# Splitting the first two modulation rows into four column blocks, and moving first-chunk layer-norm work between ScalarE and VectorE, in a fused adaLN, linear-attention and SwiGLU kernel

## The chip, the cores and the metric

The kernel runs on one core of one Trainium2 chip. The time is the device time of the core in microseconds (us). A kernel is executed several times, and the medians below are over its executions. "Granted clock" is the profile's figure for the share of the full TensorE clock that was granted on average over an execution.

## The reference

The reference is a transformer block with adaptive layer norm on 2048 tokens of width 1024, in bf16. Only the beginning matters here: six modulation rows come from the condition vector `c`, and the first two of them (shift `sa` and scale `ca`) must be known before any attention projection can start.

```
mod = (silu(c) @ w_mod).reshape(1, 6, 1, -1)        # w_mod: 1024 x 6144
sa, ca, ga, sb, cb, gb = mod[:, 0], ..., mod[:, 5]
h = layernorm(x) * (1 + ca) + sa                     # 2048 x 1024
q, k, v = h @ wqkv                                   # 32 heads of 32
... linear attention, @ wo, residual; second layer norm; SwiGLU with F = 3584; residual
```

## The kernel before

All weights are read from memory while the kernel runs. The first chunk of 512 tokens is normalised and transposed on chip; one scale and shift then make it ready for the K projection. The 1024 input channels are eight "channel rows" of 128 (`cc` 0 to 7). The modulation values of a channel row need that row's 128 columns of `w_mod` for both kinds (scale and shift). So the columns are loaded in blocks of channel rows (`PH`), interleaved with the matching rows of the K weights, and the K matmuls of the first chunk follow the blocks as they land. They accumulate in eight PSUM banks at once (`bank[0]` to `bank[7]`), one bank for each group of 128 tokens x 512 columns.

```python
PH = [(0, 2), (2, 5), (5, 8)]                     # blocks of 256, 384, 384 columns
for st in range(STC): load_x(st)
load_wme(0, 0, DC); load_wk(0, 2)                 # modulation block 0, K weights of rows 0, 1
load_wme(1, 0, 4); load_wme(1, 4, 8); load_wk(2, 3); load_wk(3, 5)
load_wme(2, 0, 4); load_wme(2, 4, 8); load_wk(5, 6); load_wk(6, 8)
...                                               # then the V weights (load_cols(wv, ...))

def mod_mm(p, kind, j0, j1):                      # one-column matmuls into columns of bank 7
    ... nc.tensor.matmul(bank[7][:, o:o + 1], lhsT=wme[:, j, col:col + P], rhs=scT[:, j:j + 1], ...)

def phi_to(dst, acc):                             # eviction of one K bank
    nc.scalar.activation(out=e, in_=acc, func=ACT.Exp)
    nc.vector.tensor_scalar(out=e, in0=e, scalar1=1.0, scalar2=PHI_EPS, op0=ALU.min, op1=ALU.add)
    nc.vector.scalar_tensor_tensor(out=dst, in0=acc, scalar=0.0, in1=e, op0=ALU.max, op1=ALU.add)

# ... front: statistics of tiles 0 to 2 on VectorE, tile 0 normalised on ScalarE, then
kblk(range(4), 0)                                 # K matmuls of groups 0..3, channel row 0
tr0(2); tr0_evac(2)                               # transpose of tile 2
# ...
kblk(range(7), 2); kblk(range(7), 3); kblk(range(3), 4)
mod_mm(2, 0, 0, 4); mod_mm(2, 1, 0, 4)
kblk(range(3, 7), 4)
mod_mm(2, 0, 4, 8); mod_mm(2, 1, 4, 8)
mod_finish(2); modulate_phase(2)                  # VectorE: casts, then scale and shift
for cc in range(5): kblk((7,), cc)                # group 7 uses bank 7, free only now
for g in range(8):
    for cc in range(5, 8): kblk((g,), cc)         # three matmuls finish each group
    k_evac(bank[g], *G[g])
# then the V groups, which use banks 0, 1, 2, ... in turn
```

## Time and profile before

| | kernel before |
|---|---|
| median, first three runs | 838.97 us (837.6 to 840.78) |
| span of the profiled run, granted clock | 836.1 us, 1.000 |
| first K matmul | 11.63 us |
| first V matmul | 30.84 us |
| TensorE gaps after 30.84 us | none until the last instructions |

Two lines of the page: the busy times of the engines, and the granted clock in 40 slices.

```profile
PE 829.2 (99%) x4208; PEld 388.7 (46%) x4208; DVE 351.3 (42%) x660; ACT 149.9 (18%) x284; POOL 79.2 (9%) x146
PEclk9999999999999999999999999999999999999999
```

TensorE is the bottleneck. From V's first matmul on it is never without work, so the span is V's start plus a constant of about 805.3 us. Only the first 31 us can change. The timeline of TensorE there follows (start, duration, line, operation; in brackets the idle time and what ended it). L267 are the K matmuls, L363 the one-column modulation matmuls, L282 the V matmuls.

```profile
11.63 1.04 PE L267 MATMUL bank<-M,M 128*128 128x512 bf16 x4 [0.25 <-DVE M L249]
...
15.23 0.82 PE L267 MATMUL bank<-M,M 128*128 128x512 bf16 x3 [0.23 <-DVE M L249]
...
17.69 3.84 PE L267 MATMUL bank<-M,M 128*128 128x512 bf16 x17 [0.24 <-DVE M L249]
21.37 0.74 PE L363 MATMUL bank<-scT,M 128*128 128x1 bf16 x24
21.98 1.02 PE L267 MATMUL bank<-M,M 128*128 128x512 bf16 x4
22.84 0.44 PE L363 MATMUL bank<-scT,M 128*128 128x1 bf16 x12
23.81 0.45 PE L363 MATMUL bank<-scT,M 128*128 128x1 bf16 x12 [0.53 <-DMA M<-in_w_mod_dram]
24.58 6.42 PE L267 MATMUL bank<-M,M 128*128 128x512 bf16 x29 [0.32 <-DVE saT L370]
30.84 13.98 PE L282 MATMUL bank<-M,M 128*128 128x512 bf16 x64
```

After the first K matmul the bracketed waits sum to 1.32 us (0.23 + 0.24 + 0.53 + 0.32). The 0.53 is the wait for the last transfer of the third modulation block, which the chain shows from its issue to its landing (start, duration, what):

```profile
14.77 8.99 DMA M<-in_w_mod_dram
```

Between 21.37 and 24.58 us TensorE is issued 48 one-column matmuls and only four K matmuls.

### The profile page before, as it was taken

To read this page: it belongs to the slowest core of one execution; us is meant where nothing else is said; L and a number is where in the kernel's file an instruction comes from. 1 tells how busy PE (TensorE), PEld (TensorE's weight loads), DVE (VectorE), ACT (ScalarE), POOL (GpSimd) and SP (SyncE) were. 2 spreads that over 40 slices of the span, in tenths; PEclk is the share of its full clock that TensorE was granted. 3 is DMA by queue.
4 is the path that set the end of the run, shared out by engine and by line. 5 is a ranking of instruction groups with operands and counts; after the bars stand their busy time and mean duration, and the time that the engine had idled before them with its cause. 6 is when DMAs were issued, how large, how long until landed. Compare 5 with 4: busy or idle time off the path is not lost.

```text
span 836.1 us, 10576 instructions
## 1 busy us (share of the span) xinstructions
PE 829.2 (99%) x4208; PEld 388.7 (46%) x4208; DVE 351.3 (42%) x660; ACT 149.9 (18%) x284; POOL 79.2 (9%) x146
## 2 busy tenths in 40 slices
PE   8999999999999999999999999999999999999998
PEld 4454544544444444444444444444444444444445
DVE  5758889788656655344552012222101111111111
ACT  3335533313211111111110001111000111100000
POOL 2114300032222223100000000000000000000000
PEclk9999999999999999999999999999999999999999
DMA  9985688154599998998884225555312555211220
GB/s 303 310 184 128 123 174 217 44 133 126 151 215 217 221 230 201 245 283 239 251 267 118 76 73 154 154 155 151 104 66 94 152 153 153 74 38 45 76 70 26
DMA packets 230529, 129.41 MB, mean 155 GB/s; under 512 B 87632, under 2 KB 216656, under 8 KB 230480
## 3 DMA queue, kind: packets, MB, share of 16 engines
q1 hardware_dynamic: 180128, 97.01, 42.2%
q10 hardware_dynamic: 48048, 23.34, 13.0%
q0 software_dynamic: 2304, 8.39, 2.6%
q8 instruction: 33, 0.54, 0.3%
q14 instruction: 16, 0.13, 0.1%
HBM read 95.42 MB, written 12.58 MB: 129 GB/s over the span
## 4 chain that ended last, share of the span: by engine, by line
PE 97%; SPq 2%; DMA 1%; issue 0%; DVE 0%
PE bank L563 23%; PE bank L538 23%; PE bank L544 23%; PE bank L282 7%; PE bank L495 7%; PE bank L290 7%; PE bank L267 6%; DMA M<-in_w_mod_dram 1%; SPq L144 1%; PE bank L468 1%; PE bank L299 1%; SPq L147 0%; SPq L137 0%; PE bank L363 0%; DVE M L566 0%
## 5 line engine op out<-in xcount | busy, mean ns | idle before, releaser
L544 PE MATMUL bank<-M,M 128*128 128x512 bf16 x896 | 211.7, 379 | 0.0
L538 PE MATMUL bank<-M,M 128*128 128x512 bf16 x896 | 211.6, 379 | 0.0
L546 DVE TENSOR_TENSOR M<-bank,e 128x512 bf16<-128x512 f32 x112 | 77.4, 691 | 249.2 <-PE bank L544 244.6
L563 PE MATMUL bank<-M,M 128*128 128x512 bf16 (+2 forms) x728 | 148.0, 363 | 0.0
L541 ACT ACTIVATE e<-bank 128x512 f32<-128x512 f32 x112 | 66.8, 597 | 439.7 <-PE bank L538 409.5
L563 PEld LDWEIGHTS <-M 128*128 128x128 bf16 x952 | 90.9, 98 | 103.0
L544 PEld LDWEIGHTS <-M 128*128 128x128 bf16 x896 | 87.7, 98 | 105.7
L538 PEld LDWEIGHTS <-M 128*128 128x128 bf16 x896 | 87.4, 98 | 103.8
L566 DVE TENSOR_TENSOR M<-bank,M 128x512 bf16<-128x512 f32 (+2 forms) x34 | 22.4, 660 | 169.9 <-PE bank L563 169.9
L267 PE MATMUL bank<-M,M 128*128 128x512 bf16 x256 | 57.4, 379 | 1.0 <-DVE M L249 0.7
L495 PE MATMUL bank<-M,M 128*128 128x512 bf16 x256 | 57.9, 379 | 0.0
L290 PE MATMUL bank<-M,M 128*128 128x512 bf16 x256 | 57.5, 379 | 0.0
L282 PE MATMUL bank<-M,M 128*128 128x512 bf16 x256 | 55.9, 379 | 0.0
L262 ACT ACTIVATE e<-bank 128x512 f32<-128x512 f32 x64 | 37.7, 595 | 86.4 <-PE bank L290 53.0
L563 PE MATMUL bank<-M 128*128 128x512 bf16 x224 | 51.0, 379 | 0.0
L264 DVE SCALAR_TENSOR_TENSOR M<-bank,e 128x512 bf16<-128x512 f32 x64 | 44.3, 692 | 3.9
L322 DVE CUSTOM_DVE_ANT_0 M<-M,sc_bc 128x1024 f32<-128x1024 bf16 x32 | 40.0, 1249 | 0.5
L282 PEld LDWEIGHTS <-M 128*128 128x128 bf16 x256 | 25.0, 98 | 30.2
L495 PEld LDWEIGHTS <-M 128*128 128x128 bf16 x256 | 25.0, 98 | 29.7
L267 PEld LDWEIGHTS <-M 128*128 128x128 bf16 x256 | 24.4, 98 | 29.6 <-DVE M L249 1.8
L263 DVE TENSOR_SCALAR e<-e 128x512 f32<-128x512 f32 x64 | 28.4, 444 | 23.0 <-ACT e L262 22.9
L290 PEld LDWEIGHTS <-M 128*128 128x128 bf16 x256 | 24.6, 98 | 27.8
(72 smaller groups left out, 337.7 us busy)
## 6 DMA issues: line engine op xcount, KB each, us to landing
M<-in_B_w_gate_dram SPq DMA_DIRECT2D x56, 512.0 KB, 3.9
M<-in_B_w_up_dram SPq DMA_DIRECT2D x56, 512.0 KB, 5.0
x_scratch<-M POOLq DMA_DIRECT2D x16, 512.0 KB, 6.0
M<-x_scratch ACTq DMA_DIRECT2D x16, 512.0 KB, 3.5
M<-in_B_w_down_dram SPq DMA_DIRECT2D x6, 1024.0 KB, 8.4
M<-in_A_x_dram SPq DMA_DIRECT2D x16, 256.0 KB, 3.6
M<-in_A_wqkv_dram SPq DMA_DIRECT2D x4, 1024.0 KB, 11.4
M<-in_A_x_dram ACTq DMA_DIRECT2D x16, 256.0 KB, 4.2
```

Of the source, the lines that this page charges most:

```text
L262: nc.scalar.activation(out=e[:], in_=acc, func=ACT.Exp)
L264: nc.vector.scalar_tensor_tensor(out=dst, in0=acc, scalar=0.0, in1=e[:], op0=ALU.max, op1=ALU.add)
L267: nc.tensor.matmul(acc[:], lhsT=M4[:, sc_, cc, t * P:(t + 1) * P], rhs=wk[:, cc, h * NB:(h + 1) * NB], start=(cc == 0), stop=(cc == DC - 1))
L282: nc.tensor.matmul(acc[:], lhsT=M4[:, sc_, cc, t * P:(t + 1) * P], rhs=wv[:, cc, h * NB:(h + 1) * NB], start=(cc == 0), stop=(cc == DC - 1))
L290: nc.tensor.matmul(acc[:], lhsT=wq[:, cc, qc * P:(qc + 1) * P], rhs=M4[:, sc_, cc, :], start=(cc == 0), stop=(cc == DC - 1))
L322: nc.vector.tensor_tensor_reduce(out=prod.rearrange("p (j k) -> p j k", j=DC), in0=rowT[i][:, :, b, :], in1=sc_bc[:].rearrange("p (j k) -> ...
L495: nc.tensor.matmul(acc[:], lhsT=oTs[st % 3][:, cc, :], rhs=wo[:, cc, hs], start=(cc == 0), stop=(cc == DC - 1))
L538: nc.tensor.matmul(g_ps[:], lhsT=wg_blk[:, cc, fs], rhs=M4[:, sc_, cc, :], start=(cc == 0), stop=(cc == DC - 1))
L541: nc.scalar.activation(out=sg[:], in_=g_ps[:], func=ACT.Silu)
L544: nc.tensor.matmul(u_ps[:], lhsT=wu_blk[:, cc, fs], rhs=M4[:, sc_, cc, :], start=(cc == 0), stop=(cc == DC - 1))
L546: nc.vector.tensor_tensor(out=gus[sc_][:, f, :], in0=u_ps[:], in1=sg[:], op=ALU.mult)
L563: nc.tensor.matmul(y_ps[:, 0:w], lhsT=gus[sc_][:, f, t * P:(t + 1) * P], rhs=wd(f)[:, c0:c1], start=(f == 0), stop=(f == FC - 1))
```

## The change: intent and diff

The last block that must arrive before K can end is made small: four blocks of 256, 384, 256 and 128 columns instead of three of 256, 384, 384. Then only one channel row, eight matmuls, remains behind it. In front, the statistics of tile 1 go to ScalarE and tile 0 is normalised on VectorE (tiles 1 to 3 already were), so that tile 2 can be transposed before the first K matmul. The bytes moved are the same.

```diff
-    PH = [(0, 2), (2, 5), (5, 8)]
+    PH = [(0, 2), (2, 5), (5, 7), (7, 8)]
@@ loads
     load_wk(5, 6)
-    load_wk(6, 8)
+    load_wk(6, 7)
+    load_wme(3, 0, DC)
+    load_wk(7, 8)
@@ front (warm(19) became warm(21))
-    for st in range(3):
-        ln_stats(st)
-    ln_xn(0)
+    ln_stats(0)
+    ln_stats_act(1)
+    ln_stats(2)
+    ln_xn(0, nc.vector)
     tr0(0)
     tr0_evac(0)
     warm(2)
-    ln_xn(1, nc.vector)
+    ln_stats(3, lambda: ln_xn(1, nc.vector))     # between the two halves
     tr0(1)
     tr0_evac(1)
-    ln_stats(3)
+    ln_xn(2, nc.vector)
     mod_mm(0, 0, 0, DC)
     mod_mm(0, 1, 0, DC)
-    warm(3)
     mod_finish(0)
+    tr0(2)
+    tr0_evac(2)
     modulate_phase(0, 0, 2 * P)
-    for st in (2, 3):
-        ln_xn(st, nc.vector)
+    ln_xn(3, nc.vector)
@@ K of the first chunk (order of the second block's part cut here)
     kblk(range(7), 2)
     kblk(range(7), 3)
-    kblk(range(3), 4)
     mod_mm(2, 0, 0, 4)
     mod_mm(2, 1, 0, 4)
-    kblk(range(3, 7), 4)
+    kblk(range(4), 4)
     mod_mm(2, 0, 4, 8)
     mod_mm(2, 1, 4, 8)
     mod_finish(2)
     modulate_phase(2)
+    kblk(range(4, 7), 4)
+    kblk(range(7), 5)
+    kblk(range(4), 6)
+    mod_mm(3, 0, 0, DC)
+    mod_mm(3, 1, 0, DC)
+    mod_finish(3)
+    modulate_phase(3)
     spread(nc.vector, scT[:])
-    for cc in range(5):
+    kblk(range(4, 7), 6)
+    for cc in range(7):
         kblk((7,), cc)
     for g in range(8):
-        for cc in range(5, 8):
-            kblk((g,), cc)
+        kblk((g,), 7)
         k_evac(bank[g], *G[g])
```

More of the change, by code (lines that the diff above doesn't have):

```diff
@@ L196, with ln_stats @@
     stat = {}
-    def ln_stats(st):
+    def ln_stats(st, between=None):
         x_sb = xs[st % 6]
@@ L201, in ln_stats @@
         for i in range(NH):
+            if i == 1 and between is not None:
+                between()
             nc.vector.bn_stats(out=stats[:, i, :], in_=x_sb[:, i * NB:(i + 1) * NB])
@@ L378, in modulate_phase @@
             modulate(0, cc, saT, ca1T, c0, c1)
-    warm(19)
+    warm(21)
     mask = const.tile([P, KVW], BF16, name="mask")
@@ L417 @@
     kblk(range(4), 0)
-    tr0(2)
-    tr0_evac(2)
-    kblk(range(2), 1)
+    kblk(range(1), 1)
     tr0(3)
     tr0_evac(3)
-    kblk(range(2, 4), 1)
+    kblk(range(1, 4), 1)
     modulate_phase(0, 2 * P, 4 * P)
+    kblk(range(4, 6), 0)
     mod_mm(1, 0, 0, 4)
     mod_mm(1, 1, 0, 4)
-    kblk(range(4, 7), 0)
+    kblk(range(6, 7), 0)
+    kblk(range(4, 5), 1)
     mod_mm(1, 0, 4, 8)
@@ L431 @@
     modulate_phase(1)
-    kblk(range(4, 7), 1)
+    kblk(range(5, 7), 1)
     kblk(range(7), 2)
     kblk(range(7), 3)
-    kblk(range(3), 4)
     mod_mm(2, 0, 0, 4)
     mod_mm(2, 1, 0, 4)
-    kblk(range(3, 7), 4)
+    kblk(range(4), 4)
     mod_mm(2, 0, 4, 8)
```

## The prediction

> **What bounds the kernel.** The busy times give TensorE 829.2 of 836.1 us; the clock is 1.00. The timeline shows no TensorE gap after 24.58 us, where the last key (K) matmuls of the first chunk begin; V begins at 30.84. The change touches only the time before that. It pays one for one if V starts earlier, and nothing otherwise.
>
> There, three limits alternate. (1) DMA: busy share 1.08 to 1.10 in every 5 us window from 5 to 25; transfers land in queue order: first modulation block 10.11, first K weights 11.48, second block 16.28, third 23.76, first V weights 28.78 us. (2) The chain "last modulation matmul, casts, modulate on VectorE, K matmul": 16.64 to 17.69, 1.05 us. (3) TensorE itself: from 11.63 to 30.84 it has 64 K matmuls of 0.216, two transposed tiles (0.9) and 96 small matmuls (2.5): 17.2 of 19.2 us. Only some 2 us are waits, so that is the ceiling; one more tile transposed before 11.63 could add 0.45.
>
> **What the change does.**
> - Bytes are unchanged, packets shorter. Medians in the trace: 768 B take 40 ns, 512 B 27 ns, 256 B (transposing loads elsewhere) 18 ns. The third block falls to 1 MB at 512 B, about 3.4 us (estimate); the last, 0.5 MB at 256 B, about 2.1 us against 1.6 at 768 B. [...] Estimates: third block 22.5 (was 23.76), fourth 26.0, last K weights 26.7, V weights 29.7 us (was 28.78).
> - Front: normalising tile 0 on VectorE (0.54 us) for ScalarE (1.24) waits behind tile 2's statistics, so it ends near 7.5 instead of 7.66. Tile 1's statistics on ScalarE take 1.05+0.2+0.2+1.15+0.2, then three POOL steps of 1.3: ready near 8.5, as now. The first K matmul stays near 11.6, because its weights land at 11.48. Little is gained.
> - Middle: tile 3's copy and modulate now leave TensorE about 0.7 us idle near 14; the small matmuls that filled this come later. Third channel block: 17.85 instead of 17.69.
> - End: 18 instead of 29 matmuls follow the last modulation matmuls, but these come near 26.5 instead of 24.2. K ends near 30.5.
> - New: the final row is one matmul per group (0.216) instead of three (0.65), so bank 0 finishes only near 29.1 us; its exp, min/add and max/add take 1.8 us (26.50 to 28.28 before). V's first group uses bank 0, so V starts near 31.0. The eight evictions end near 38.4 instead of 35.7, on VectorE, with slack: the second chunk's modulation ended 3 us before it was needed.
>
> Thus the waits removed (about 1) are paid back by this eviction and new waits. Net +0.2 us by the sum, with an error of 0.6; small against the runs' spread (837.6 to 840.78).
>
> **Prediction: 838.9 us, range 836.9 to 841.0. Faster by over 2%: 0.005; within 2%: 0.985; slower: 0.01.**
>
> **Right if** the profile shows: first K matmul 11.4 to 11.8; the fourth block landing 25.5 to 26.7; V weights 29.3 to 30.3; V's first matmul 30.3 to 31.3, after a short wait for bank 0's eviction; no TensorE waits later; no more ScalarE table loads than now.
>
> **Wrong if** 256 B packets cost far more than 18 ns (each us moves V's start); if Copy and Square need a table load (1.28 us), delaying tile 1; if the later eviction delays the second chunk's transposes enough to stop TensorE near 60 us; or if the small matmuls fill waits better than I count, giving a start near 29.7 (1 us faster).

The transfer times of 3.4, 2.1 and 1.6 us are estimates; the packet medians beside them give much the same over the 16 DMA engines of the page (2048 x 27 ns, 2048 x 18 ns and 683 x 40 ns, divided by 16: 3.5, 2.3 and 1.7 us).

## The result and the profile after

| | before | after |
|---|---|---|
| median of six runs | 839.39 us (837.6 to 840.78) | 838.2 us (838.03 to 838.74) |
| span of the profiled run, clock | 836.1 us, 1.000 | 837.0 us, 1.000 |
| first K matmul | 11.63 us | 11.51 us |
| first V matmul | 30.84 us | 31.44 us |

The ratio after to before is 0.999, with a 95% interval of 0.9976 to 1.0004: the same. Ratios in this document are the mean time of one kernel's fast runs over that of the other's in the same rounds, so they are not quite the ratios of the medians.

There is a contradiction to explain. The median fell by 1.2 us, but the profiled run became 0.9 us longer, 0.6 us of it because V starts later. First the profile. The page's busy times, then TensorE's timeline; L271 are now the K matmuls, L367 the one-column matmuls, L286 the V matmuls. (Some matmul records are missing from the trace, so counts can be short by a few.)

```profile
PE 825.1 (99%) x4127; PEld 388.4 (46%) x4207; DVE 351.5 (42%) x660; ACT 150.9 (18%) x288; POOL 80.1 (10%) x147
```

```profile
11.51 1.25 PE L271 MATMUL bank<-M,M 128*128 128x512 bf16 x4 [0.32 <-DVE M L253]
...
14.45 0.61 PE L271 MATMUL bank<-M,M 128*128 128x512 bf16 x2 [0.59 <-DVE M L253]
...
17.59 1.69 PE L271 MATMUL bank<-M,M 128*128 128x512 bf16 x7 [0.46 <-DVE M L253]
19.75 1.67 PE L271 MATMUL bank<-M,M 128*128 128x512 bf16 x7 [0.48 <-DMA M<-in_A_wqkv_dram]
21.26 0.54 PE L367 MATMUL bank<-scT,M 128*128 128x1 bf16 x16
21.66 1.02 PE L271 MATMUL bank<-M,M 128*128 128x512 bf16 x4
22.52 0.81 PE L367 MATMUL bank<-scT,M 128*128 128x1 bf16 x16
23.41 0.59 PE L271 MATMUL bank<-M,M 128*128 128x512 bf16 x2
24.24 2.55 PE L271 MATMUL bank<-M,M 128*128 128x512 bf16 x11 [0.24 <-DVE M L253]
26.63 0.54 PE L367 MATMUL bank<-scT,M 128*128 128x1 bf16 x16
27.03 4.04 PE L271 MATMUL bank<-M,M 128*128 128x512 bf16 x18
31.44 13.76 PE L286 MATMUL bank<-M,M 128*128 128x512 bf16 x61 [0.36 <-DVE M L268]
```

The wait for the modulation transfer (0.53 us) is gone, and the K matmuls behind the last block fell from 29 to 18. But the waits after the first K matmul now sum to 2.13 us (0.59 + 0.46 + 0.48 + 0.24 + 0.36). Some of these have other causes than before: 0.59 us for tile 3's scale and shift, which 24 one-column matmuls had filled before; 0.48 us for K weights whose slowest part landed at 19.71 us (19.04 before); and 0.36 us between K and V. The chain of waits shows what the last one is (start, duration, what):

```profile
14.85 8.09 DMA M<-in_w_mod_dram
...
29.60 0.61 ACT e L266
30.23 0.44 DVE e L267
...
30.69 0.70 DVE M L268
...
31.44 0.59 PE bank L286 x2
```

These three instructions are the eviction of bank 0 (the reading of its finished sums), the bank that V's first group needs. In the kernel before it ran from 26.50 to 28.28 us, under K matmuls. Now each group is finished by a single matmul in the last row, so bank 0 is finished only near 29.6 us. Its eviction takes 1.8 us and ends after K does.

The trace's completion times of the transfers answer the other part of the prediction: third block 22.93 us, fourth block 26.04, V weights 29.67 (28.78 before). The packets of 256 bytes took 18 ns in the median, those of 512 bytes 27 ns.

### The profile page after: what moved, and what is told of

The parts are those of the page before. It is cut to its first block, busy times and chain, and to the rows that moved or that the text cites. A ratio compares the mean times of both kernels' runs of the same rounds, so it can differ in the third digit from the quotient of the medians.

```text
span 837.0 us, 10504 instructions
## 1 busy us (share of the span) xinstructions
PE 825.1 (99%) x4127; PEld 388.4 (46%) x4207; DVE 351.5 (42%) x660; ACT 150.9 (18%) x288; POOL 80.1 (10%) x147
## 4 chain that ended last, share of the span: by engine, by line
PE 96%; SPq 2%; DMA 1%; issue 1%; DVE 0%; ACT 0%
PE bank L555 23%; PE bank L574 23%; PE bank L549 23%; PE bank L286 7%; PE bank L506 7%; PE bank L294 7%; PE bank L271 6%; DMA M<-in_w_mod_dram 1%; PE bank L479 1%; PE bank L303 1%; SPq L144 1%; SPq L147 1%; SPq L137 0%; PE bank L367 0%; DVE M L268 0%
## 5 line engine op out<-in xcount | busy, mean ns | idle before, releaser
L577 DVE TENSOR_TENSOR M<-bank,M 128x512 bf16<-128x512 f32 (+2 forms) x34 | 22.5, 661 | 169.9 <-PE bank L574 153.8
L271 PE MATMUL bank<-M,M 128*128 128x512 bf16 x248 | 56.8, 379 | 2.6 <-DVE M L253 1.6
L286 PE MATMUL bank<-M,M 128*128 128x512 bf16 x251 | 55.6, 379 | 0.6 <-DVE M L268 0.4
L286 PEld LDWEIGHTS <-M 128*128 128x128 bf16 x256 | 25.0, 98 | 30.8 <-issue 0.6
L271 PEld LDWEIGHTS <-M 128*128 128x128 bf16 x256 | 24.1, 98 | 30.8 <-DVE M L253 3.3
L294 PEld LDWEIGHTS <-M 128*128 128x128 bf16 x256 | 24.6, 98 | 27.9
```

What stands on the lines that cost most here:

```text
L271: nc.tensor.matmul(acc[:], lhsT=M4[:, sc_, cc, t * P:(t + 1) * P], rhs=wk[:, cc, h * NB:(h + 1) * NB], start=(cc == 0), stop=(cc == DC - 1))
L286: nc.tensor.matmul(acc[:], lhsT=M4[:, sc_, cc, t * P:(t + 1) * P], rhs=wv[:, cc, h * NB:(h + 1) * NB], start=(cc == 0), stop=(cc == DC - 1))
L294: nc.tensor.matmul(acc[:], lhsT=wq[:, cc, qc * P:(qc + 1) * P], rhs=M4[:, sc_, cc, :], start=(cc == 0), stop=(cc == DC - 1))
```

## The experiments

Twelve kernels ran, in three sessions of four, each on another chip, called A, B and C here. Five executions were asked for each, beside nine of the kernel before in the same session; every execution has its own mean granted clock. One question is where V starts, which one profile for each kernel answers for that execution: two profiles of one kernel differ by 0.03 to 0.32 us (before and e8_before, after and e11_after, e1_tail and e12_tail). The other is why the executions of one kernel differ by up to 3 us.

| profiled run | V starts, us | span, us | span minus V's start |
|---|---|---|---|
| before | 30.84 | 836.1 | 805.3 |
| after | 31.44 | 837.0 | 805.6 |
| e1_tail | 30.23 | 835.8 | 805.6 |
| e2_front | 32.49 | 838.7 | 806.2 |
| e3_blocks | 31.03 | 836.5 | 805.5 |
| e4_noblock4 | 31.38 | 836.5 | 805.1 |
| e5_fill | 32.07 | 837.3 | 805.2 |
| e6_starve | 31.30 | 837.7 | 806.4 |
| e7_best | 30.98 | 837.3 | 806.3 |
| e8_before | 30.90 | 836.1 | 805.2 |
| e9_small | 39.26 | 844.7 | 805.4 |
| e10_large | 33.74 | 839.0 | 805.3 |
| e11_after | 31.41 | 836.9 | 805.5 |
| e12_tail | 30.55 | 836.1 | 805.6 |

In eleven of fourteen profiles the last column is 805.1 to 805.6 us: the start of V sets the time one for one. Compared weight load by weight load, TensorE in the kernel after is 0.60 us behind the kernel before at 33 us, and still 0.60 us at 830 us. In the three others (e2, e6, e7) TensorE lost 0.8 to 1.0 us near 168 us by the same comparison, at the numerator and denominator matmuls of the attention. What starts that wait was not looked into; it comes with early and with late starts of V.

### Session A: what sets V's start (e1 to e4)

**e1_tail**: the kernel after, with group 7's matmuls moved behind the last row of the other groups.

```diff
     kblk(range(4, 7), 6)
-    for cc in range(7):
+    for cc in range(2):
         kblk((7,), cc)
-    for g in range(8):
+    for g in range(7):
         kblk((g,), 7)
         k_evac(bank[g], *G[g])
+    for cc in range(2, 8):
+        kblk((7,), cc)
+    k_evac(bank[7], *G[7])
```

> The kernel after, with one edit: six of the eight K matmuls of the last group (bank 7) go behind the last matmuls of the groups 0 to 6, so that bank 0 is finished and its eviction begins earlier; the number of matmuls is the same. Theory A (V's first matmul waits for bank 0's eviction, and the whole time moves with V's first matmul): bank 0 is free near 30.3 us, TensorE goes from K to V without a gap, V starts 30.9 to 31.1 us (31.44 now), the span falls by 0.3 to 0.5 us. Rival B (transfers set V's start): V starts at 31.4 still. Rival C (the 1 us between the kernels is noise of the rest of the run): V's start moves but the time does not follow.

Median 838.16 us (837.59 to 838.66; the slowest run has a clock of 0.998), ratio to before 0.9989 (0.9977 to 1.0002). TensorE's timeline at the end of K:

```profile
25.94 0.54 PE L367 MATMUL bank<-scT,M 128*128 128x1 bf16 x16
26.34 4.04 PE L271 MATMUL bank<-M,M 128*128 128x512 bf16 x18
30.23 4.05 PE L286 MATMUL bank<-M,M 128*128 128x512 bf16 x17
```

The gap in front of V is gone. V starts earlier than expected, but not all of that belongs to the edit, since the transfers also came on time in this run. The clean measure is the time from the last one-column matmuls to V: 30.23 - 25.94 = 4.29 us here, 31.44 - 26.63 = 4.81 us in the kernel after. The late eviction of bank 0 cost 0.52 us. Theory A holds.

**e2_front**: the front of the kernel after, with the blocks, loads and end of the kernel before.

```diff
-    PH = [(0, 2), (2, 5), (5, 7), (7, 8)]
+    PH = [(0, 2), (2, 5), (5, 8)]
   # loads as before; from the third block on, the K order of the kernel before
```

> The front of the kernel after (tile 1's statistics on ScalarE, four tiles normalised on VectorE, third tile transposed early, its K order up to the second block) with the three blocks and the end of the kernel before. Theory A: first K matmul 11.4 to 11.7, third channel row 17.5 to 17.8, V starts 30.6 to 31.0, as before: the front is worth at most 0.2 us, for the weights' landing (11.4) and the second block's landing (16.2) set it. Rival D (the front is the useful part of the change): V starts by 30.3 or earlier.

Median 838.08 us (837.88 to 840.47), ratio 0.9989 (0.9975 to 1.0002). First K matmul 11.62, third channel row 17.70, and the last stretch of K starts at 24.55 us, against 24.58 before. So the new front gained nothing up to there, as theory A has it. But V started at 32.49 us, which neither theory had expected. This run took 840.47 us. It is taken up below.

**e3_blocks**: the reverse, the old front with the four blocks.

```diff
-    PH = [(0, 2), (2, 5), (5, 8)]
+    PH = [(0, 2), (2, 5), (5, 7), (7, 8)]
   # loads as after; from the third block on, the K order of the kernel after
```

> The front of the kernel before with the four blocks and the end of the kernel after. Theory A: V starts 31.2 to 31.7, about where the kernel after has it, because its end is the same and bank 0's eviction (1.8 us after its last matmul) ends it; first V matmul preceded by a gap of 0.3 to 0.6 us. Rival D: V starts at least 0.5 us later than in the kernel after.

Median 838.37 us (838.27 to 838.6), ratio 0.9993 (0.998 to 1.0005). V started at 31.03 us after a gap of 0.36 us for bank 0's eviction, a little earlier than the expected range. The old front is not worse than the new one: rival D falls.

**e4_noblock4**: the kernel after without the fourth block's transfer; the small matmuls of the last channel row read the columns of the row before it. It is wrong, yet the comparison with the reference still passed, so that comparison is blind to an error in one of eight channel rows' modulation.

```diff
-    load_wme(3, 0, DC)
-                col = (0 if kind else D) + cc * P
+                col = (0 if kind else D) + min(cc, 6) * P
```

> The kernel after without the transfer of the fourth modulation block (0.5 MB in packets of 256 B); its small matmuls read the columns of channel row 6 in place of 7, so the result is wrong on purpose. Every later transfer lands 1.2 to 1.5 us earlier. Theory A (TensorE's order and bank 0's eviction set V's start): V starts 31.0 to 31.4, at most 0.3 us earlier. Rival B (the transfers, with short packets, set V's start): V starts near 30.1, 1.2 us or more earlier.

Median 838.02 us (837.84 to 839.08), ratio 0.9991 (0.9978 to 1.0003). V started at 31.38 us, 0.06 us earlier than after, and again 4.81 us after the last one-column matmuls. Half a megabyte less changed nothing: at the end of K the transfers do not bind, and the short packets of the fourth block cost nothing on the critical path. Rival B falls:

```profile
26.57 0.54 PE L366 MATMUL bank<-scT,M 128*128 128x1 bf16 x16
31.38 2.97 PE L285 MATMUL bank<-M,M 128*128 128x512 bf16 x12 [0.36 <-DVE M L267]
```

### What the slow executions are

Session A gave the clock of every execution. The nine of the kernel before:

```
us     837.65 837.75 837.88 838.68 | 838.83 839.34 839.71 839.73 840.38
clock  1.0    1.0    1.0    1.0    | 0.998  0.998  0.998  0.998  0.998
```

The slowest five are those with a granted clock of 0.998. A share of 0.002 of 837 us is 1.7 us. Where in those five runs it was lost is not recorded. The e2_front profile caught such a run. Here are its windows, cut at the changes of its clock record (columns: busy times of PE, PEld, DVE, ACT and POOL with instruction counts; then the granted clock, DMA share and GB/s), and its timeline:

```profile
18.07:21.48 3.41, 3.41 (x22) 1.57 (x19) 0.21 (x1) 0.00 (x0) 0.00 (x0) 1.00 1.10 329
21.48:24.89 3.41, 2.59 (x54) 1.82 (x53) 0.59 (x4) 0.00 (x0) 0.00 (x0) 1.00 1.07 366
24.89:28.30 3.41, 3.28 (x9) 1.22 (x8) 1.44 (x4) 0.44 (x1) 0.00 (x0) 0.50 1.10 365
28.30:31.71 3.41, 3.41 (x17) 1.54 (x16) 3.12 (x7) 2.86 (x6) 0.00 (x0) 1.00 1.06 362
```

```profile
21.38 0.74 PE L365 MATMUL bank<-scT,M 128*128 128x1 bf16 x24
21.98 1.02 PE L269 MATMUL bank<-M,M 128*128 128x512 bf16 x4
22.84 0.44 PE L365 MATMUL bank<-scT,M 128*128 128x1 bf16 x12
23.77 0.45 PE L365 MATMUL bank<-scT,M 128*128 128x1 bf16 x12 [0.49 <-DMA M<-in_w_mod_dram]
24.55 8.11 PE L269 MATMUL bank<-M,M 128*128 128x512 bf16 x28 [0.32 <-DVE saT L372]
32.49 3.83 PE L284 MATMUL bank<-M,M 128*128 128x512 bf16 x17
```

For exactly one period of 3.41 us, from 24.89 us, the clock is half. In it K matmuls start every 0.43 us instead of every 0.216 us, and the 6.42 us of the kernel before become 8.11 us: V starts 1.65 us later. The period before it, 21.48 to 24.89 us, is the stretch noted above, of one-column matmuls and few large ones. The page counts TensorE as busy for 2.59 of those 3.41 us, and the longest wait is 0.49 us. So no long idle time stood before the fall of the clock to 0.50.

This leads to theory H, a supposition, which is still to be tested here: what counts is how much the array works in a period, not whether TensorE is issued to, and the stretch from 21.4 to 24.6 us is poor enough to halve the next period if the periods' phase lies badly. (The phase differs between profiles: counted in steps of 3.41 us along the clock record, a period begins at 21.48 us here, at 20.99 us in the kernel before and at 21.11 us in the kernel after.) Its rival, that the busy time of a period decides, whatever the matmuls are, had no run of its own, but two traces speak against it. In e2_front the period from 11.24 to 14.65 us is busy for only 2.38 us by the page, less than the 2.59 us of the punished one. In e9_small below, the period from 7.90 to 11.31 us is busy for 2.43 us. Both hold large matmuls and transposes, and after both the clock stayed at 1.00.

### Session B: the frequency of slow runs (e5 to e8)

**e5_fill**: three idle-filling matmuls in the wait of the kernel before.

```diff
+    def fill(n):
+        for _ in range(n):
+            nc.tensor.matmul(bank[7][:, 16:NB], lhsT=zt[:, 0:P], rhs=zt[:, 0:NB - 16], start=False, stop=True, ...)
     mod_mm(2, 0, 4, 8)
+    fill(3)
     mod_mm(2, 1, 4, 8)
```

> The kernel before with one addition: three idle-filling matmuls (zeros, into 496 unused columns of bank 7) while TensorE waits for the last transfer of the third modulation block, near 23.1 us. Theory H (the kernel before loses 1 to 2 us in about half of its executions because TensorE's clock is halved for one period of 3.41 us after a period, 21 to 24.6 us, that holds only some five large matmuls): the busy share of that period rises from 0.31 to about 0.5, V starts at 30.8 as before, and no run shows a granted clock of 0.998: all five take 837.5 to 838.2 us, the median falls by about 1 us against the kernel before. Rival N (the slow runs are chance, nothing to do with this stretch): two or three of the five runs are at 839 us or more with clock 0.998, as in the kernel before.

**e6_starve**: the kernel after with the stretch made poor.

```diff
-    kblk(range(4), 4)
     mod_mm(2, 0, 4, 8)
     mod_mm(2, 1, 4, 8)
+    kblk(range(4), 4)
```

> The kernel after with one edit: four K matmuls that stand between the two halves of the third block's small matmuls are moved behind them. The period from 21 to 24.5 us then holds only some five large matmuls, as in the kernel before. Theory H: two or more of the five runs show clock 0.998 and take 839 us or more (none of six did in the kernel after); the undisturbed runs stay at 838.0 to 838.4. Rival N: no or one run is disturbed, as in the kernel after.

**e7_best**: e1_tail with the second block's first one-column matmuls moved into the wait near 14 us, and five filling matmuls in later waits.

```diff
-    kblk(range(4, 6), 0)
     mod_mm(1, 0, 0, 4)
     mod_mm(1, 1, 0, 4)
-    kblk(range(6, 7), 0)
-    kblk(range(4, 5), 1)
+    kblk(range(4, 7), 0)
     mod_mm(1, 0, 4, 8)
+    kblk(range(4, 6), 1)
+    fill(1)
     mod_mm(1, 1, 4, 8)
     # ... then kblk(range(6, 7), 1); fill(3) ... and fill(1) after kblk(range(4, 7), 4)
```

> The tail order of e1_tail, the small matmuls of the second block back in the idle time near 14 us, and five idle-filling matmuls where TensorE waits (near 16, 17 and 23 us). Theories A and H together: V starts 29.9 to 30.4 us, no run with clock 0.998, all runs 837.2 to 837.9, faster than both kernels' medians by 0.5 to 1.5 us.

**e8_before**: the kernel before, unchanged.

> The kernel before once more, unchanged, to count its slow runs. Theory H: two or more of five runs near 839.5 us with clock 0.998, the others near 837.8 with clock 1.0, and little in between; if the profiled run is a slow one, its clock record shows one halved period that begins near 24.5 us and V starts near 32.5. Rival N: a slow run's record shows halved periods elsewhere.

Not one of the nine executions of the kernel before beside them, nor of the five of e8_before, had a clock under 1.0 on this chip; they took 837.63 to 838.54 us. The expectation of two or more slow runs was wrong. The same kernel had 0.998 in five of nine executions on chip A and in none of these fourteen, so how often it happens does not depend on the kernel alone. So these runs say little about H: e5_fill (838.13 us, clocks 1.0) had nothing to cure; its runs took up to 839.05 us, and V started at 32.07 us instead of 30.8. The chain to it begins at the K weights of rows 3 and 4, which landed at 20.28 us (19.04 in the kernel before); a share of the fill in it was not separated. e6_starve (839.4 us, clocks 1.0) was not struck either, against the expectation. Nor did its edit make the stretch as poor as planned: its poorest 3.41 us hold 1.78 us of K matmuls, those of the kernel before's profile 1.39 us. It was slower than the kernel before for reasons that its profile shows: V starts 0.40 us later than in e8_before, and about 0.9 us are lost near 168 us.

e7_best failed as a best version: 838.83 us, ratio 1.0009 (0.9995 to 1.0023). In its profile V started at 30.98 us instead of 29.9 to 30.4, right after V's weights had landed (30.94 us; 29.67 in the kernel after), and it too lost time near 168 us.

### Session C: provoking it, and a direct comparison (e9 to e12)

**e9_small** and **e10_large** lengthen the poor stretch of the kernel before by the same 3.6 us, once with 140 one-column matmuls, once with 17 matmuls of 496 columns.

```diff
     mod_mm(2, 0, 4, 8)
+    fill_small(140)      # e9: bank[7][:, 16:17], one column each
+    fill(17)             # e10 instead: bank[7][:, 16:512]
     mod_mm(2, 1, 4, 8)
```

> The kernel before with 140 matmuls of one column (25.6 ns each, 3.6 us; zeros into an unused column of bank 7) put between the small matmuls of the third modulation block, so that TensorE is issued to without a rest but has only some five large matmuls in 6.8 us, twice a clock period. Theory H: at least one period of 3.41 us holds almost no large matmul, whatever the phase, so in every run the next period is granted half the clock (mean clock 0.998 or lower in the records of most runs), and V starts 2.9 us later than before for the added time and up to 1.7 us more for the halved clock: 33.6 to 35.5 us. Rival N (TensorE that is issued to without idle time keeps its clock): no halved period, V starts at 33.6 to 34.0 as in e10_large.

> The same place and about the same added time (17 matmuls of 496 columns, 0.21 us each, 3.6 us) as in e9_small, but the array works. Theory H: no halved period in the record, clock 1.0 in all runs, V starts 33.6 to 34.0 us, the runs within 0.7 us of each other, at 840.5 to 841.3. Rival N: like e9_small.

e9_small gave four runs: 845.99, 846.27, 846.43 and 847.69 us, with clocks of 0.994 to 0.996. e10_large: median 840.73 us, four of five runs with clock 1.0, one of 842.95 us with 0.998. The nine runs of the kernel before beside them had a clock of 1.0. First the windows of e9_small, with the same columns as above, then the timeline of e10_large. The trace of e10_large has no clock record (its page lacks the line PEclk, so the 1.00 that the windows print for it, and probably the 1.0 listed for this run, are no measurements), so its clock is read from the pace of the matmuls:

```profile
21.56:24.97 3.41, 3.33 (x85) 2.53 (x85) 0.00 (x0) 0.00 (x0) 0.00 (x0) 1.00 1.05 366
24.97:28.38 3.41, 2.68 (x108) 2.62 (x105) 0.00 (x0) 0.00 (x0) 0.00 (x0) 1.00 1.09 366
28.38:31.79 3.41, 1.04 (x10) 0.65 (x11) 1.16 (x6) 0.00 (x0) 0.00 (x0) 0.50 1.07 364
31.79:35.21 3.42, 3.42 (x9) 1.18 (x9) 0.97 (x3) 0.60 (x1) 0.00 (x0) 0.50 1.10 349
```

```profile
23.17 3.72 PE L198 MATMUL bank<-M 128*128 128x496 bf16 x17
27.49 6.42 PE L272 MATMUL bank<-M,M 128*128 128x512 bf16 x28 [0.32 <-DVE saT L375]
33.74 4.48 PE L287 MATMUL bank<-M,M 128*128 128x512 bf16 x20
```

The period from 24.97 to 28.38 us of e9_small holds 108 small and no large matmuls. TensorE is busy for 2.68 us of it by the page, yet the next period gets half the clock. In e10_large, large matmuls stand in the same place, and no halving shows: the last stretch of K takes 6.42 us, as in the kernel before, with a matmul every 0.216 us. That is H's core, shown on a chip where the kernel before was not struck once.

V started 5.52 us later in e9_small than in e10_large (39.26, where 33.6 to 35.5 was expected, against 33.74). From the first K matmul of the last stretch to V it took 8.38 us (30.88 to 39.26) against 6.25 (27.49 to 33.74): 2.1 us from the halved clock. Most of the rest was not foreseen. TensorE stopped in the middle of the one-column matmuls, from 27.65 to 30.21 us, waiting for nothing that the profile shows:

```profile
30.21 0.35 PE L368 MATMUL bank<-scT,M 128*128 128x1 bf16 x8 [2.56 <-issue]
```

A packet of 16 KB on the queue that the profile calls instruction started at 27.76 us and took 1.11 us. Whether the stop has to do with it was not tested. The stop also left the second period poor, so the second halving may be its work. The first is hardly so: only 0.7 us of the period before it fell into the stop, and the period from 7.90 to 11.31 us, with even less busy time but with large matmuls in it, was not punished.

Two things stay open. One run of e10_large had a clock of 0.998 against the expectation, and no trace of it exists. And how poor a period must be is not shown: counting K matmuls alone, TensorE was busy for 1.42 of 3.41 us in the period that was punished in e2_front, for 1.57 us in the nearest period of the kernel before's profile (20.99 to 24.40 us), and for 1.41 us in the first period shown of e9_small; the last two went unpunished. So this count alone does not decide a borderline case.

**e11_after** and **e12_tail** are the kernel after and e1_tail again, beside the kernel before on one chip.

> The kernel after once more, beside the kernel before on one chip. Theories A and H: undisturbed runs of the kernel after are 0.2 to 0.7 us slower than undisturbed runs of the kernel before (V starts 31.0 to 31.5 against 30.8); only if the kernel before has runs with clock 0.998 here is its mean the higher one. Rival D (the change gains 1 us by itself): undisturbed runs of the kernel after are 0.5 us or more faster.

> e1_tail once more, on the chip of e11_after. Theory A: V starts 30.2 to 31.0, no gap before it, and the median of undisturbed runs is 0.3 to 0.8 us below the kernel after and 0 to 0.5 us below the kernel before.

| chip C, all clocks 0.999 or 1.0 | median, us | range | ratio to before (95%) |
|---|---|---|---|
| before, nine runs | 837.85 | 837.42 to 838.76 | |
| e11_after, five runs | 838.23 | 838.01 to 838.71 | 1.0004 (0.9992 to 1.0017) |
| e12_tail, five runs | 837.93 | 837.82 to 838.02 | 1.0 (0.9988 to 1.0013) |

Undisturbed, the kernel after is not faster than the kernel before; the medians have it 0.4 us slower, inside the interval. V's start agrees: 31.41 us after a gap of 0.36 us. The tail edit brings V to 30.55 us (4.29 us after the last one-column matmuls, as in session A) and the median back to that of the kernel before. No version here beats both kernels clearly.

## Why the prediction was right, and where it was not

The measured 838.2 us lies in the range of 836.9 to 841.0 us, and the sum behind it named the right parts. That the number fits says little: the range is some 4 us wide, far more than the change could do either way by the sum, and it starts from a median of three runs of which two (838.97 and 840.78 us) were probably slow ones. The profile tests more. Point by point:

- **First K matmul at 11.4 to 11.8 us, little gained in front.** 11.51 us; and e3_blocks, with the old front, started V at 31.03 us, not later than the kernel after. One term was wrong without effect: tile 0 was normalised at 7.98 us, not near 7.5, since the statistics of tile 2 had to wait 0.38 us for its data.
- **Transfers.** Third block expected at 22.5, fourth at 26.0, V weights at 29.7 us; they landed at 22.93, 26.04 and 29.67. The 18 ns for 256 bytes held. The shorter packets moved less in their time: 14 bytes per ns at 256 bytes (256/18), 19 at 512 (512/27). But e4_noblock4 shows that this transfer is not on the critical path.
- **Idle time near 14 us of about 0.7 us.** 0.59 us. The third channel row came at 17.59 us instead of 17.85. A wait of 0.48 us for the K weights of rows 3 and 4 was not foreseen; they landed at 19.71 us, in six other profiles with the same loads (e1, e3, e6, e7, e11, e12) between 18.75 and 19.67.
- **V waits for bank 0's eviction.** Shown: a gap of 0.36 us in the profile, removed in e1_tail, where the tail costs 0.52 us less.
- **V starts 30.3 to 31.3 us (about 31.0).** Slightly missed on the late side: 31.44 and 31.41 us. The mis-sized term is the end of bank 0's row. The last one-column matmuls came at 26.63 us, nearly as expected (26.5), and the eviction took the expected 1.8 us, but bank 0 was finished near 29.6 instead of 29.1 us: 3.0 us after those matmuls, where the sum had 2.6. From them to V it took 4.81 us in after, e3, e4, e6 and e11 alike, where the sum had 4.5. The unforeseen wait for K weights explains little of the miss: it acts through those last one-column matmuls, and they were only 0.13 us late.
- **No new table loads.** Right: ScalarE has two loads of 1.28 us in the first 45 us in both traces. In the kernel after they begin at 1.18 us (before Silu) and at 12.26 us (before Exp); Copy (4.33 us) and Square (5.75 us) ran between them without a load of their own.
- **Evictions end near 38.4 us with slack.** They ended at 38.79 us, and TensorE had no gap near 60 us.
- **Net +0.2 us.** On one chip, with no halved clock, the medians differ by +0.4 us (838.23 against 837.85), which the interval does not tell from zero.

What the prediction lacked is the reason for "the runs' spread (837.6 to 840.78)", which it took as noise. On chip A it was not noise: the five slowest of nine runs of the kernel before had a clock of 0.998, a loss as large as that of one halved period (0.002 of 837 us is 1.7 us), and these runs took about 1 to 2.7 us longer than the three fastest. The first comparison, too, had four of six runs of the kernel before at 838.97 to 840.78 us and two at 837.6 to 837.74; the six runs of the kernel after, with clocks of 0.999 and 1.0, lay within 0.7 us. So the 1.2 us by which the median fell are probably a matter of which runs were struck. The clocks of those six runs of the kernel before are not recorded, so this is argued, not shown. Nor is it shown that the change makes the kernel safer. It does put more large matmuls into the poor stretch (K matmuls busy for 2.21 us of the period from 21.11 to 24.52 us in its profile, against 1.57 us before), and none of its eleven runs had 0.998. But it was never run on chip A. There the kernels with the old stretch (before and e2_front) had 0.998 in six of fourteen runs, and those with the four blocks (e1_tail, e3_blocks, e4_noblock4) in one of fifteen: a run of e1_tail, 838.66 us. That points to a safer kernel, on one chip and in few runs.

## What to carry to other kernels

When a pipeline is fed by transfers, making the last piece small also makes the last row of work small: ask which eviction was hidden under the work that is no longer there (here bank 0's, which cost 0.52 us), and order that row so that the first bank the next stage needs is finished first. Look at the clock of every execution before a spread of 0.3% is called noise; in e2_front one period of 3.41 us at half the clock brought V 1.65 us later. A stretch of one-column matmuls can look busy on the page and be followed by half the clock all the same: in e9_small 108 of them made TensorE busy for 2.68 of 3.41 us, and the next period had 0.50, while in e10_large, with 17 matmuls of 496 columns in that place, the K matmuls behind kept their 0.216 us. Large matmuls between the small ones may thus help; they lower the risk at most, since one of five runs of e10_large had 0.998. And see that a clock was recorded at all before a printed 1.00 is believed.
